# Lightning attention and a PReLU MLP on one core: converting transfers for q of chunk 1, and a new order of the whole list of calls

## The chip, the cores and the metric

The kernel runs on one core of one Trainium2 chip. The metric is device time in microseconds (us). Three runs of the kernel before took 202.56, 203.06 and 203.26 us, a median of 203.06.

The engines are named as in the profile: PE is TensorE (matrix products and transposes), with PEld for its weight loads; DVE is VectorE, ACT is ScalarE, POOL is GpSimd, and SP is the engine that only issues transfers here. PSUM is the memory that PE writes its products to; the other memory on the core is SBUF.

## What is computed

The reference has two parts. The first is linear attention with a decay for each head, in blocks of 64 positions, for 4 batches, 8 heads, 768 positions and a head dimension of 64. The result, x, has 3072 rows of 512, and goes through a two-layer MLP (512 to 2048 to 512) with a PReLU whose slope is given for each of the 2048 columns.

```python
for b in range(nb):                                   # blocks of 64 positions
    intra = einsum('bhic,bhjc->bhij', qb, kb) * Dmask[None]
    intra = einsum('bhij,bhjd->bhid', intra, vb)
    inter = einsum('bhid,bhde->bhie', qb * lam_pow[None], kv_state)
    out[:, :, sl] = intra + inter
    kb_dec = kb * rev_pow[None]
    kv_state = lam_block * kv_state + einsum('bhsd,bhse->bhde', kb_dec, vb)
...
h = x @ w_in
g = np.maximum(h, 0.0) + alpha * np.minimum(h, 0.0)
return (g @ w_out).astype(np.float32)
```

The inputs and the output are of 32-bit floats; the kernel multiplies in 16 bits.

## The kernel before, in words

**Tiles.** The rows are cut into six chunks, c = 0 to 5. A chunk holds 256 positions of two batches, 512 rows of x. Its attention is done in four units, one for each batch `bi` and half of the heads `hh`; so there are 24 units, and units 4c to 4c+3 make chunk c. Blocks are taken 128 positions at a time, two in a unit.

**A unit of attention** goes through these steps, each a small function:
- q, k and v are loaded. `load` (L89) brings q or k as 32-bit numbers into a raw tile, from the queue of SP or, with "G", of GpSimd; `cast` (L247 on ACT, L249 on DVE, L251 on GpSimd) makes 16 bits of it. `load_q16` (L279) and `load_v16` (L288) are converting transfers on GpSimd's queue, which read 32-bit numbers and write 16-bit ones, so that no cast is needed. `load_q16` puts a unit's q into its tile with the heads in another order.
- q and k are transposed. For units 0 to 8 PE does it (`turn`), into a bank of PSUM, and `turn_copy` copies the bank to `qkT` (L247 on ACT, L249 on DVE). Where q came by `load_q16`, `turn` does a unit's q with eight transposes of 64 columns (L334), else with four of 128 (L336). For units 9 to 23 a transfer on SP's queue transposes (`turned`).
- `key_decayed` multiplies k by its decay: one instruction on DVE or GpSimd (L308), or eight on ACT (L306), one for each head and parity. `decayed` (L361) does the same for q.
- `score_products` (L397, 16 small products) writes the scores into the one buffer `s` in PSUM; `masked` (L408, DVE) multiplies them by the mask of decays into `sm`, which frees `s`. `intra` (L422) multiplies them by v, `inter` (L381) multiplies q by the state, both into `acc`. `state_products` (L442), or `state_in` (L492 and L442) in a bank of its own, makes the next state's sum, and `first_state` (L469, ACT) or `states` (L477, DVE, two instructions for each block) adds it to the decayed state.
- `attended` copies `acc` to the tile xT (L247 on ACT, L249 on DVE), where the MLP reads it.

**The MLP.** `up(c, f)` (L518) multiplies w_in by a chunk's xT, for one of 16 groups f of 128 columns, into one of four banks of PSUM: four products of 512 columns, or of 256 where only one batch is ready (`up(0, 4, 0)`). `relu` (L531, ACT) makes relu(-h), and `prelu` or `prelu_half` (L546, DVE) adds it, times 1 - alpha, to h, which gives g in 16 bits. For chunk 0 `down` (L554) is the plain second product. For chunks 1 to 5 the second product is done in the manner of Strassen, in seven products instead of eight (`second`, L675, 256 columns each, tile names y and b), which need sums and differences of quarters of g (`g_sum`) and w_out (`w_sum`). For chunks 4 and 5 the up product is done the same way, as they are taken together (`first`, L800, tile names a, e and b), with sums of w_in (`in_sum`) and of the two chunks' xT (`x_sum`, i = 1 to 4, for each of two groups of rows). All these sums are one instruction each on L593 (a difference) or L596 (a sum), on DVE or, with "G", on GpSimd. `first(f, 5)` needs `x_sum(1, ...)`, which needs the first half of the heads only, unit 22 at the latest.

**The order.** All is called from one list, written out by hand from line 819 on: 1079 calls, each of which issues its instructions at once. Every engine runs its own instructions in the order of the list, and waits where data or a buffer isn't ready. `vector_turn(n)` marks the newest DVE instruction, and `gpsimd_waits(n)` makes the newest GpSimd instruction wait for that mark. `fill` (L133, 512 columns) and `tick` (L145, 128 columns) are products that nobody reads, ahead of the first transposes. The list ends with the second products of chunks 4 and 5.

```python
def turn(n, xs):                       # cut
    ...
        if x == 0 and "q16" in t:
            for l in range(2):
                nc.tensor.transpose(tp[ds(64 * l, 64), i, e, hp, :], t["q16"][:, 2 * hp + l, e], ident)
            continue
        nc.tensor.transpose(tp[:, i, e, hp, :], t["qk16"][:, x, e, ds(2 * hp, 2)]..., ident)
```

Of the kernel before, what the change touches and what calls it, by code (L numbers as in the profile page):

```python
# [11 lines left out]
def kernel(  # L12
# [489 lines left out]
    G = {}  # L502
# [316 lines left out]
    query_decay(3, 1)  # L819
    query_decay(2, 1)  # L820
    mask_logs(2)
    tick(6)
    load_q16(2)
    mask_logs(0)
    key_decay()
    state_decay()
    load(0, 0, "k", None)
    load(0, 1, "k", None)
    cast(0, "k16", "V")
    query_decay(0, 1)  # L830
    load_q16(0)
    load_q16(1)
    key_decayed(0, "V")
    mask_logs(1)
    key_decayed(1, "V")
    decay_mask(2)
    decay_mask(0)
    cast(1, "k16", "V")
    vector_turn(0)
    tick(56)  # L840
    load_q16(3)
    load_v16(1)
    decay_mask(1)
    mask_logs(3)
    query_decay(1, 1)
    turn(1, (1,))
    turn_copy(1, (1,), "V")
    decay_mask(3)
    query_decay(0, 0)
    load_alpha()  # L850
    load_v16(0)
    turn(1, (0,))
    turn_copy(1, (0,), "V")
    load_v16(2)
    turn(0, (1,))
    turn_copy(0, (1,), "V")
    turn(0, (0,))
    turn_copy(0, (0,), "A")
    load_v16(3)
    load_win(1)  # L860
    slopes_turn()
    slopes()
    load_win(0)
    decayed(1, "P")
    score_products(1)
    masked(1)
    fill(3)
    key_decayed(2)
    gpsimd_waits(0)
    cast(2, "k16", "A")  # L870
    turn(2, (0,))
    turn_copy(2, (0,), "V")
    state_in(1, 0)
    first_state(1)
    decayed(2)
    cast(3, "k16", "A")
    decayed(0)
    score_products(0)
    masked(0)
    turn(2, (1,))  # L880
    turn_copy(2, (1,), "A")
    key_decayed(3)
    inter(1)
    intra(1)
    attended(1, "A")
    load_win(3)
    turn(3, (0,))
    turn_copy(3, (0,), "A")
    state_in(0, 0)
    first_state(0)  # L890
    load(1, 0, "q", 0, "G")
    score_products(2)
    masked(2)
    turn(3, (1,))
    turn_copy(3, (1,), "A")
    state_in(2, 0)
    first_state(2)
    decayed(3)
    load(1, 0, "k", 0, "G")
    load(1, 0, "q", 1, "G")  # L900
    load_win(2)
    inter(0)
    intra(0)
    attended(0, "A")
    load_v16(4)
    load(1, 0, "k", 1, "G")
    state_in(1, 1)
    states(1, (1,))
    load_wout(0)
    score_products(3)  # L910
    masked(3)
    state_in(3, 0)
    first_state(3)
    inter(2)
    intra(2)
    attended(2, "A")
    load(1, 1, "q", 1, "G")
    state_in(2, 1)
    states(2, (1,))
    state_in(3, 1)  # L920
    states(3, (1,))
    state_in(0, 1)
    states(0, (1,))
    cast(4, "q16", "G")
    inter(3)
    intra(3)
    attended(3, "A")
    up(0, 4, 0)
    relu(0, 4, 0)
    up(0, 5)  # L930
    up(0, 3)
    up(0, 6)
    prelu_half(0, 4, 0)
    relu(0, 5)
    relu(0, 3)
    prelu(0, 5)
    up(0, 7)
    relu(0, 6)
    up(0, 13)
    prelu(0, 3)  # L940
    up(0, 15)
    relu(0, 7)
    prelu(0, 6)
    relu(0, 13)
    turn(4, (0,))
    relu(0, 15)
    prelu(0, 7)
    up(0, 14)
    load(1, 1, "k", 1, "G")
    prelu(0, 13)  # L950
    turn_copy(4, (0,), "A")
    up(0, 1)
    relu(0, 14)
    prelu(0, 15)
    cast(4, "k16", "G")
    turn(4, (1,))
    load_v16(5)
    load_wout(1)
    up(0, 0)
    prelu(0, 14)  # L960
    cast(5, "q16", "A")
    up(0, 4, 1)
    turn_copy(4, (1,), "A")
    relu(0, 1)
    relu(0, 4, 1)
    cast(5, "k16", "G")
    load(1, 1, "q", 0, "G")
    up(0, 9)
    key_decayed(4, "V")
    state_products(4, None, True)  # L970
    in_sum(1, 1, "G")
    score_products(4)
    load_wout(2)
    prelu(0, 1)
    prelu_half(0, 4, 1)
    relu(0, 0)
    relu(0, 9)
    turn(5, (0,))
    cast(7, "q16", "G")
    up(0, 12)  # L980
    relu(0, 12)
    first_state(4)
    load_wout(3)
    prelu(0, 0)
    w_sum(1, 1, "G")
    decayed(4)
    up(0, 2)
    turn_copy(5, (0,), "V")
    relu(0, 2)
    turn(5, (1,))  # L990
    prelu(0, 9)
    up(0, 11)
    relu(0, 11)
    prelu(0, 12)
    prelu(0, 2)
    key_decayed(5)
    turn_copy(5, (1,), "V")
    up(0, 8)
    gate(2, "out")
    prelu(0, 11)  # L1000
    load(1, 1, "k", 0)
    relu(0, 8)
    up(0, 10)
    prelu(0, 8)
    down(0, 2, 0)
    down(0, 0, 0)
    states(4, (1,))
    inter(4)
    masked(4)
    relu(0, 10)  # L1010
    down(0, 3, 0)
    intra(4)
    score_products(5)
    cast(6, "q16", "A")
    cast(7, "k16", "G")
    decayed(5)
    state_products(5)
    prelu(0, 10)
    w_sum(1, 3)
    in_sum(1, 2)  # L1020
    vector_turn(1)
    turn(7, (0,))
    load_v16(7)
    load_v16(6)
    first_state(5)
    down(0, 2, 1)
    in_sum(1, 3, "G")
    gpsimd_waits(1)
    turn_copy(7, (0,), "V")
    w_sum(2, 3, "G")  # L1030
    down(0, 3, 1)
    load_v16(8)
    states(5, (1,))
    attended(4, "A")
    decayed(7, "V")
    vector_turn(2)
    load(2, 0, "k", 0)
    turn(6, (0,))
    turn_copy(6, (0,), "V")
    w_sum(1, 0)  # L1040
    masked(5)
    down(0, 0, 1)
    w_sum(2, 1)
    turn(7, (1,))
    inter(5)
    w_sum(4, 1)
    key_decayed(7, "V")
    decayed(6, "V")
# [879 lines left out]
```

## Time and profile before

| | us |
|---|---|
| median of three runs | 203.06 (202.56 to 203.26) |
| the profiled execution, its own time | 203.85 |
| its span, first to last instruction | 202.1 |
| PE busy | 194.8, 96% of the span |
| DVE busy | 171.8, 85% |
| POOL busy | 142.1, 70% |
| ACT busy | 130.1, 64% |
| granted clock of TensorE, mean | 0.999 of full speed |

The busy times overlap, and PE's weight loads (130.0) run beside its products. In a row of a timeline stand the start in us from the span's start, the length, the engine, the line, the operation, the tiles written and read, their sizes and types, and the number of instructions joined in the row; a bracket tells how long the engine had stood idle just before, and which instruction the profile takes for the one that ended it. In a row of the waits stand the engine and line that waited, the engine and line waited for, the sum, the number of times and the longest. In the chain stand start, length and what ran. In a row of the groups by line stand, behind the bar, the busy time of the group and the mean length of one instruction in ns, and then the idle time before it with what ended most of it. In a row of the transfers stand their number, the size of each, and the median time from issue to landing.

### The profile page before, as it was taken

To read this page: it belongs to the slowest core of one execution; us is meant where nothing else is said; L and a number is where in the kernel's file an instruction comes from. 1 tells how busy PE (TensorE), PEld (TensorE's weight loads), DVE (VectorE), ACT (ScalarE), POOL (GpSimd) and SP (SyncE) were. 2 spreads that over 40 slices of the span, in tenths; PEclk is the share of its full clock that TensorE was granted. 3 is DMA by queue.
4 is the path that set the end of the run, shared out by engine and by line. 5 is a ranking of instruction groups with operands and counts; after the bars stand their busy time and mean duration, and the time that the engine had idled before them with its cause. 6 is when DMAs were issued, how large, how long until landed. Compare 5 with 4: busy or idle time off the path is not lost.

```text
span 202.1 us, 5896 instructions
## 1 busy us (share of the span) xinstructions
PE 194.8 (96%) x2367; PEld 130.0 (64%) x2367; DVE 171.8 (85%) x319; ACT 130.1 (64%) x279; POOL 142.1 (70%) x160
## 2 busy tenths in 40 slices
PE   7997999999999999999999999998999999999992
PEld 7965454556545688666556667655666656788891
DVE  6887789869989999899999998899989999895800
ACT  5585686336977799687768588364596986633022
POOL 8989959773889839999999989870476222656700
PEclk9999999999999999999999999999999999999999
DMA  5999999999989999999996935110040001113143
GB/s 156 199 198 230 239 260 234 200 278 235 235 127 248 228 199 238 164 280 142 262 207 161 185 26 136 67 63 0 2 156 3 0 2 54 55 34 122 55 143 117
DMA packets 60991, 30.01 MB, mean 149 GB/s; under 512 B 31700, under 2 KB 60004, under 8 KB 60964
## 3 DMA queue, kind: packets, MB, share of 16 engines
q1 hardware_dynamic: 41236, 19.87, 40.7%
q0 software_dynamic: 19568, 9.70, 36.1%
q8 instruction: 18, 0.29, 0.6%
q14 instruction: 9, 0.07, 0.1%
q10 hardware_dynamic: 160, 0.07, 0.1%
HBM read 27.27 MB, written 6.29 MB: 166 GB/s over the span
## 4 chain that ended last, share of the span: by engine, by line
PE 91%; DVE 4%; ACT 3%; issue 0%; ACTq 0%; DVEq 0%
PE h_ps L518 27%; PE y L675 16%; PE b L675 12%; PE o_ps L554 7%; PE b L800 5%; PE acc L422 4%; PE s L397 3%; PE a L800 3%; PE e L800 3%; PE unread L145 3%; PE acc L381 2%; PE tp L336 2%; PE acc L442 1%; DVE x L593 1%; ACT xT L247 1%; PE tp L334 1%
## 5 line engine op out<-in xcount | busy, mean ns | idle before, releaser
L518 PE MATMUL h_ps<-xT,w_in_sb 128*128 128x512 f16 (+1 forms) x264 | 59.5, 373 | 1.0 <-DVE g L546 1.0
L675 PEld LDWEIGHTS <-g 128*128 128x128 f16 x464 | 44.6, 98 | 10.5 <-DVE g L593 1.1
L546 DVE SCALAR_TENSOR_TENSOR g<-m,oma,h_ps 128x512 f16<-128x512 f32 (+1 forms) x66 | 46.1, 727 | 4.9 <-ACT m L531 3.5
L531 ACT ACTIVATE m<-h_ps 128x512 f32<-128x512 f32 (+1 forms) x66 | 37.4, 582 | 16.5 <-PE h_ps L518 15.6
L518 PEld LDWEIGHTS <-w_in_sb 128*128 128x128 f16 x264 | 24.5, 98 | 26.2 <-DVE g L546 1.3
L408 DVE TENSOR_TENSOR sm<-s,dmask 128x1024 f16<-128x1024 f32 x24 | 29.3, 1219 | 1.5 <-PE s L397 1.4
L675 PE MATMUL y<-w_out_sb,g 128*128 128x256 f16 x224 | 27.9, 273 | 0.6 <-DVE g L593 0.6
L593 POOL TENSOR_TENSOR g<-g 128x512 f16<-128x512 f16 x11 | 13.2, 1204 | 16.0 <-DVE s L596 15.9
L361 POOL TENSOR_TENSOR qdT<-qkT,qdecay 128x512 f16<-128x512 f16 (+1 forms) x20 | 20.8, 1043 | 3.2 <-DMA qkT<-qk 1.2
L675 PE MATMUL b<-t,g 128*128 128x256 f16 x160 | 19.8, 273 | 0.0
L288 POOL DMA_DIRECT2D v<-in_v_dram x24 | 18.6, 783 | 0.0
L247 ACT ACTIVATE xT<-acc 128x512 f16<-128x512 f32 x22 | 13.1, 595 | 8.2 <-PE acc L442 5.1
L593 POOL TENSOR_TENSOR g<-g,g 128x512 f16<-128x512 f16 x12 | 14.1, 1190 | 5.5 <-DVE g L593 3.3
L477 DVE SCALAR_TENSOR_TENSOR R<-R,rdecay,acc 128x128 f16<-128x128 f16 x54 | 15.6, 342 | 2.8 <-ACT xT L247 2.2
L596 POOL TENSOR_TENSOR s<-g,g 128x512 f16<-128x512 f16 x9 | 10.4, 1158 | 8.4 <-DVE g L546 8.4
L554 PE MATMUL o_ps<-w_out_sb,g 128*128 128x512 f16 x64 | 15.3, 380 | 0.0
L247 ACT ACTIVATE o_sb<-y 128x512 f32<-128x512 f32 (+2 forms) x12 | 6.2, 526 | 13.0 <-PE y L717 7.1
L308 POOL TENSOR_TENSOR kdec<-kraw,kdecay 128x512 f16<-128x512 f32 x13 | 13.6, 1054 | 0.8 <-DVE w_out_sb L593 0.8
L306 ACT ACTIVATE kdec<-kraw,kdecay 128x64 f16<-128x64 f32 x56 | 14.0, 344 | 0.0
L251 POOL CAST qk<-kraw 128x512 f16<-128x512 f32 x10 | 6.1, 608 | 5.9 <-DMA kraw<-in_k_dram 2.4
L422 PE MATMUL acc<-sm,v 64*64 64x128 f16 x384 | 9.9, 220 | 0.1
L397 PE MATMUL s<-qkT 64*64 64x128 f16 x384 | 9.9, 219 | 0.0
(133 smaller groups left out, 368.7 us busy)
## 6 DMA issues: line engine op xcount, KB each, us to landing
out_dram<-o_sb SPq DMA_DIRECT2D x23, 256.0 KB, 2.5
kraw<-in_k_dram SPq DMA_DIRECT2D x8, 512.0 KB, 5.8
v<-in_v_dram POOLq DMA_DIRECT2D x24, 128.0 KB, 5.2
qraw<-in_q_dram SPq DMA_DIRECT2D x5, 512.0 KB, 6.5
w_in_sb<-in_moe_w_in_dram POOLq DMA_DIRECT2D x4, 512.0 KB, 7.5
w_out_sb<-in_moe_w_out_dram POOLq DMA_DIRECT2D x4, 512.0 KB, 9.4
qraw<-in_q_dram SPq DMA_DIRECT2D x6, 256.0 KB, 5.5
kraw<-in_k_dram SPq DMA_DIRECT2D x5, 256.0 KB, 4.5
```

The costliest lines, as they stand in the source:

```text
L247: nc.scalar.activation(out, in_, AF.Copy)
L288: nc.gpsimd.dma_start(out=v16.rearrange("p h e d -> p h (e d)"), in_=v[2 * (c % 2) + bi, ds(4 * hh, 4), ds((c // 2) * W, W), :].rearrange( ...
L361: engine(eng).tensor_tensor(out=qdT[:, :, :, p], in0=(t["qps"] if eng == "P" else t["qkT"][:, 0])[:, :, :, p], in1=qdecay[:, hh, :, :, p], ...
L408: nc.vector.tensor_tensor(out=t["sm"].rearrange("p a h x j -> p (a h) x j"), in0=t["s"].rearrange("p a h x j -> p (a h) x j"), in1=mask_of ...
L422: nc.tensor.matmul(ot[a][ds(hl * 64, 64), hp, :], lhsT=t["v16"][p, 2 * hp + hl, e, :], rhs=t["sm"][p, hl, hp, 1 - e, :], start=(2 * pb + a ...
L518: nc.tensor.matmul(h[:, 0:n] if bi is None else h[:, 0:n].rearrange("p (e j) -> p e j", e=2), lhsT=w_in_sb[:, gi, ts(f, 128)], rhs=x.rearr ...
L531: nc.scalar.activation(m[:, 0:n], HP[c, f, bi][:, 0:n], AF.Relu, scale=-1.0)
L546: engine(eng).scalar_tensor_tensor(out=g, in0=m, scalar=oma[:, f : f + 1], in1=h, op0=ALU.mult, op1=ALU.add)
L554: nc.tensor.matmul(O[c, t], lhsT=g_of(c, f)[:, t // 2, t % 2, :], rhs=w_out_sb[:, f, :], start=(f == 0), stop=(f == NF - 1),)
L593: engine(eng).tensor_tensor(out=out, in0=a, in1=b, op=ALU.subtract)
L675: nc.tensor.matmul(Y[c, k][:, ds(b * HALF, HALF)], lhsT=left(c, i, f, b), rhs=right(i, f), start=(f == 0 and b == 0 and i in (1, 5)), stop ...
L800: nc.tensor.matmul(t, lhsT=w, rhs=x, start=(g == 0 and i in (1, 5)), stop=(g == 1), skip_group_check=True)
```

## The change

Only the list is changed; every function is the same. It has 1078 calls for 1079.

First, q of chunk 1 (units 4 to 7). Before it came by four plain loads on GpSimd's queue and four casts, two on GpSimd and two on ACT; now by four converting transfers. `turn` then takes its other branch for these units, eight transposes of 64 columns for four of 128, 16 more on PE in all.

```diff
-    load(1, 0, "q", 0, "G")
-    load(1, 0, "q", 1, "G")
-    load(1, 1, "q", 1, "G")
-    load(1, 1, "q", 0, "G")
-    cast(4, "q16", "G")
-    cast(5, "q16", "A")
-    cast(7, "q16", "G")
-    cast(6, "q16", "A")
+    load_q16(4)
+    load_q16(7)
+    load_q16(5)
+    load_q16(6)
...
-    key_decayed(2)
-    gpsimd_waits(0)
-    cast(2, "k16", "A")
+    key_decayed(3, "V")
+    vector_turn(0)
```

Second, the order is new nearly everywhere from the first call to the second products of the last chunk, whose tail is the same on each engine. With it some work goes to other engines. On ACT `key_decayed` is done for 11 units, before for 7. On DVE the differences of L593 go from 54 to 48 and the sums of L596 from 37 to 34, on GpSimd both together from 55 to 64. DVE does five copies of `attended` and four casts, before two and three. There are 25 calls of `gpsimd_waits`, before 22, and 18 of `vector_turn`, as before.

The first place that the prediction speaks of is DVE at the first four units. L249 copies transposes (`qkT`) or makes xT (CAST), L361 is `decayed`, L408 `masked`, L308 `key_decayed`, L477 `states`, and L237 makes 1 - alpha. Before:

```order
L195 SCALAR_TENSOR_TENSOR dmask<-rel_f,loglam,drop 128x192 x2
L249 COPY qkT<-tp 128x512 x3
L237 TENSOR_SCALAR oma<-at_ps 128x16
L361 TENSOR_TENSOR qdT<-tp,qdecay 128x4x64
L408 TENSOR_TENSOR sm<-s,dmask 128x1024
L249 COPY qkT<-tp 128x512
L408 TENSOR_TENSOR sm<-s,dmask 128x1024 x2
L477 SCALAR_TENSOR_TENSOR R_1_2_101<-R_1_1_100,rdecay,kv 128x128 x2
L408 TENSOR_TENSOR sm<-s,dmask 128x1024
```

After, at the same place:

```order
L249 COPY qkT<-tp 128x512
L308 TENSOR_TENSOR kdec<-kraw,kdecay 128x512
L249 COPY qkT<-tp 128x512
L361 TENSOR_TENSOR qdT<-tp,qdecay 128x4x64
L249 COPY qkT<-tp 128x512
L408 TENSOR_TENSOR sm<-s,dmask 128x1024
L249 COPY qkT<-tp 128x512
L408 TENSOR_TENSOR sm<-s,dmask 128x1024
L249 CAST xT<-acc 128x2x4x64
L408 TENSOR_TENSOR sm<-s,dmask 128x1024
L237 TENSOR_SCALAR oma<-at_ps 128x16
L477 SCALAR_TENSOR_TENSOR R_0_2_104<-R_0_1_103,rdecay,kv 128x128 x2
```

The fourth masking is the next row in the list after. A `key_decayed` now stands between the first two copies, a copy to xT between the second and the third masking, and the slopes and a pair of states ahead of the fourth.

The second place is DVE at the last masking, of unit 23, where attention ends and the up products of chunks 4 and 5 begin. Here `g0` to `g3` are a chunk's g, `s1` to `s4` sums of w_in (or of g, for s1 on L596), and `x1`, `x2`, `x4` the sums of xT. Before:

```order
L408 TENSOR_TENSOR sm_3017<-s_2955,dmask_175 128x1024
L546 SCALAR_TENSOR_TENSOR g3_2629<-m_3020,oma_182,h_ps_3010 128x512
L593 TENSOR_TENSOR g2_2242<-g2_2242,g0_2079 128x2x256
L593 TENSOR_TENSOR x1_3071<-xT_2808,xT_2438 128x512
L593 TENSOR_TENSOR x2_3076<-xT_2808,x1_3071 128x512
L593 TENSOR_TENSOR x4_3078<-xT_2438,x2_3076 128x512
L593 TENSOR_TENSOR g3_1978<-g3_1978,g1_2035 128x2x256
L593 TENSOR_TENSOR g0_2386<-g0_2386 128x2x256
L593 TENSOR_TENSOR x2_3076<-xT_2808,x1_3071 128x512
L593 TENSOR_TENSOR g3_1978<-g3_1978,g1_2035 128x2x256
```

After:

```order
L408 TENSOR_TENSOR sm_3062<-s_3000,dmask_175 128x1024
L593 TENSOR_TENSOR s4_3064<-w_in_sb_121,s2_2030 128x512
L593 TENSOR_TENSOR x1_3066<-xT_2896,xT_2442 128x512
L593 TENSOR_TENSOR s4_3064<-w_in_sb_121,s2_2030 128x512
L596 TENSOR_TENSOR s1_1652<-g0_2489,g2_2464 128x512
L593 TENSOR_TENSOR x1_3066<-xT_2896,xT_2442 128x512
L593 TENSOR_TENSOR s4_3064<-w_in_sb_121,s2_2030 128x512
L546 SCALAR_TENSOR_TENSOR g3_2662<-m_3116,oma_182,h_ps_3068 128x512
L546 SCALAR_TENSOR_TENSOR g1_2722<-m_3079,oma_182,h_ps_3048 128x512
L593 TENSOR_TENSOR x2_3134<-xT_2896,x1_3066 128x512
```

Both halves of x1 are made on DVE now (before, one of them on GpSimd), ahead of two PReLUs and of x2; the sums of g for the second product of chunk 2 no longer stand among them. On PE, between the last `intra` and the first `first(1, 1)`, stand `second(2, 4, 1)` and `second(2, 3, 0)` now, before `second(2, 4, 1)` alone.

More of the change, by code (lines that the diff above doesn't have):

```diff
@@ L995 @@
[L995 to L1011, printed above, removed]
+    up(0, 8)
+    turn(7, (0,))
+    load_v16(6)
+    turn_copy(7, (0,), "V")
+    turn(6, (0,))
+    relu(0, 11)
     intra(4)
     score_products(5)
-    cast(6, "q16", "A")
-    cast(7, "k16", "G")
@@ L1158 @@
+    cast(11, "q16", "A")
     load_v16(12)
[L1159 to L1182 removed]
+    load(3, 1, "q", 0)
+    relu(1, 13)
@@ L1342 @@
+    up(2, 12)
+    up(2, 1)
+    states(13, (0, 1))
+    cast(18, "q16", "A")
+    second(1, 4, 0)
+    masked(13)
+    relu(2, 12)
+    relu(2, 1)
+    load_v16(19)
+    inter(13)
+    key_decayed(16, "A")
+    intra(13)
+    prelu(2, 12)
+    prelu(2, 1)
+    decayed(14)
+    load(4, 0, "q", 0)
+    state_products(14)
     score_products(14)
+    up(2, 13)
+    second(1, 4, 1)
+    masked(14)
     prelu(2, 2)
-    intra(13)
-    state_products(14)
-    relu(2, 12)
+    attended(13, "A")
+    states(14, (0, 1))
```

1656 lines of the change are left out of this document (826 added, 830 removed).

## The prediction

> **What bounds the kernel now.** I read the page's totals first, then the span in windows, then the list of waits with TensorE as the one that waits, then the chain that ended last and the timeline at the two places where TensorE waits. First the page.
>
> ```profile
> span 202.1 us, 5896 instructions
> PE 194.8 (96%) x2367; PEld 130.0 (64%) x2367; DVE 171.8 (85%) x319; ACT 130.1 (64%) x279; POOL 142.1 (70%) x160
> PE 91%; DVE 4%; ACT 3%; issue 0%; ACTq 0%; DVEq 0%
> ```
>
> TensorE (PE) is busy for 194.8 of 202.1 us and carries 91% of the chain. So a new order can win only from the 7.3 us in which PE stands, and it loses whatever matmuls it adds. The windows say where those 7.3 us lie (behind the length come the busy times of PE, of its weight loads, and of DVE, ScalarE and GpSimd).
>
> ```profile
> 0.00:5.00 5.00, 3.88 (x34) 3.59 (x35) 3.44 (x15) 2.83 (x8) 4.16 (x14) 1.00 0.55 154
> 15.00:20.00 5.00, 3.83 (x121) 2.70 (x112) 4.01 (x11) 2.71 (x6) 4.98 (x8) 1.00 1.23 223
> 110.00:120.00 10.00, 10.00 (x145) 6.91 (x143) 9.99 (x20) 7.02 (x14) 9.01 (x10) 1.00 0.71 107
> 130.00:140.00 10.00, 9.09 (x75) 5.51 (x74) 9.21 (x18) 4.85 (x10) 5.23 (x5) 1.00 0.16 54
> 196.00:202.10 6.10, 2.13 (x24) 1.79 (x21) 0.00 (x0) 1.36 (x3) 0.00 (x0) 0.96 0.34 114
> ```
>
> 1.12 us at the start, 1.17 in 15 to 20, 0.91 in 130 to 140 and 3.97 behind the last product make 7.17 of the 7.3. The start and the end belong to set-up and to the last store; the order of the first two microseconds and of the tail stays the same on each engine, so I leave both at zero. What a new list can touch is the 1.17 and the 0.91, and VectorE (DVE), which is 9.99 busy of 10 in 110 to 120 without PE yet losing anything there. The list of waits names what PE waited for in the later one; the row of the earlier one (19.37) is shown in part 2.
>
> ```profile
> PE y L675 <- DVE g L593: 0.6, 1, 0.6
> PE e L800 <- DVE x L593: 0.3, 1, 0.3
> ```
>
> **Part 1, eight short transposes for four long ones.** Units 4 to 7 are concerned; the chain has one group of each form side by side.
>
> ```profile
> 8.66 0.22 PE tp L336 x4
> 8.88 0.34 PE tp L334 x8
> 9.22 0.33 PE tp L336 x4
> ```
>
> Four of 128 columns take 0.22, eight of 64 take 0.34, so a unit costs 0.12 more, and four units 4 x 0.12 = +0.48. They stand between up-products, where PE is the bound, so nothing hides them. The other group of four took 0.33; by that one the term would be 4 x 0.01 = +0.04. I take 0.48, since 0.22 is a group that follows others without a break, and keep both ends. The four casts that go (two on GpSimd, two on ScalarE) were on engines with 30% and 36% free: nothing.
>
> **Part 2, the first units.** The list of the first four units is new. Before, it ran like this on DVE and PE.
>
> ```profile
> 6.66 0.68 DVE L308 TENSOR_TENSOR kdec<-kraw,kdecay 128x512 f16<-128x512 f32 x1
> 8.92 1.10 DVE L249 COPY qkT<-tp 128x512 f16<-128x512 f16 x3 [0.59 <-PE tp L336]
> 10.54 1.22 DVE L408 TENSOR_TENSOR sm<-s,dmask 128x1024 f16<-128x1024 f32 x1
> 12.28 1.23 DVE L408 TENSOR_TENSOR sm<-s,dmask 128x1024 f16<-128x1024 f32 x1 [0.19 <-PE s L397]
> 14.02 1.23 DVE L408 TENSOR_TENSOR sm<-s,dmask 128x1024 f16<-128x1024 f32 x1 [0.52 <-PE s L397]
> 15.46 0.61 DVE L477 SCALAR_TENSOR_TENSOR R<-R,rdecay,kv 128x128 f16<-128x128 f16 x2 [0.21 <-PE kv L442]
> 15.98 1.22 DVE L408 TENSOR_TENSOR sm<-s,dmask 128x1024 f16<-128x1024 f32 x1
> 18.82 0.48 DVE L546 SCALAR_TENSOR_TENSOR g<-m,oma,h_ps 128x256 f16<-128x256 f32 x1
> 3.28 5.37 PE unread L145 x62
> 10.41 0.75 PE unread L133 x3
> 17.48 0.38 PE acc L422 x16
> 17.88 0.60 ACT xT L247
> 19.37 1.90 PE L518 MATMUL h_ps<-xT,w_in_sb 128*128 128x512 f16 x8 [1.01 <-DVE g L546]
> ```
>
> Follow the four maskings (L408), which carry the chain there.
> - Ahead of the first transposes stand 56 small fillers and the three large ones, for 62: three large take 0.75, six small 6 x 5.37/62 = 0.52, so the first copy begins at 8.92 + 0.23 = 9.15.
> - Between the two copies of unit 1 now stands a key_decayed of unit 3, 0.68 with the next instruction 0.6 behind it. So the second copy begins at 9.15 + 0.35 + 0.6 = 10.1 (0.35 is a third of the 1.10), scores follow at 10.45 and last some 0.4. The first masking starts at about 11.15, for 10.54: +0.6.
> - The second masking waits for scores in the one buffer that the first empties; the distance of 1.74 stays: 12.9, for 12.28, +0.6.
> - Ahead of the third scores PE now has intra of unit 1, a state product and the transposes of unit 3; PE reaches them at about 14.3, not 13.6: 14.7 to 15.0, for 14.02.
> - Ahead of the fourth stand the slopes and one pair of states (0.61): 16.8 to 17.6, for 15.98, +0.8 to +1.6.
>
> Behind the fourth masking come intra (0.38), the copy to xT (0.60) and then up(0,5), the first product that needs all four units. In the trace xT ends at 17.88 + 0.60 = 18.48; up(0,5) began at 19.37, after a wait of 1.01. Moving 18.48 by 0.8 to 1.6 gives 19.3 to 20.1. So the wait that is there hides nearly the whole delay: -0.1 to +0.7, and I take the middle, +0.3. If that cover is none (the wait moves along), it is a rival below. GpSimd's loads are moved too. Of the four of w_in three are issued earlier than before, and the last, w_in(2), behind seven other issues of 0.77 each, at about 20.5 by the trace's GpSimd rows.
>
> ```profile
> w_in_sb<-in_moe_w_in_dram POOLq DMA_DIRECT2D x4, 512.0 KB, 7.5
> 16.69 0.77 POOL L89 DMA_DIRECT2D kraw<-in_k_dram x1
> ```
>
> It lands near 28.0. Its first reader, up(0,9), comes behind eleven up-products of four times 0.216 (0.86 each), so at 19.7 + 9.5 = 29.2 at the earliest: nothing, with 1.2 us of cover; if that were gone PE would stand for what is missing.
>
> **Part 3, the change from attention to the last two chunks.** Here PE lost time in two steps.
>
> ```profile
> 134.15 1.37 DVE L593 TENSOR_TENSOR x<-xT 128x512 f16<-128x512 f16 x1
> 136.90 0.42 DVE L593 TENSOR_TENSOR x<-xT,x 128x512 f16<-128x512 f16 x1
> 134.89 0.38 PE L800 MATMUL e<-x,s 128*128 128x512 f16 x1
> 135.57 0.81 PE L800 MATMUL e<-x,s 128*128 128x512 f16 x3 [0.30 <-DVE x L593]
> 136.22 0.88 PE L675 MATMUL y<-w_out_sb,g 128*128 128x256 f16 x6
> 137.71 0.39 PE L675 MATMUL y<-w_out_sb,g 128*128 128x256 f16 x2 [0.61 <-DVE g L593]
> 133.90 1.33 POOL L593 TENSOR_TENSOR s<-w_in_sb,s 128x512 f16<-128x512 f16 x1
> 31.82 2.59 PE h_ps L518 x12
> ```
>
> A product of 512 columns takes 2.59/12 = 0.216, so the second e could start at 135.11, and started at 135.57: 0.46 lost. Six of 256 columns, at half of that each, take 6 x 0.108 = 0.65, so the next y could start at 136.87, and started at 137.71: 0.84 lost. Together 1.3. After the change the sums x(1), which need only units already copied, stand on DVE directly behind the last masking and behind at most two other sums (0.42 each) apiece; the sums of g for second(2,4) are done on GpSimd and DVE ahead of them; and between the last intra and the first e PE has two groups of second products (8 x 0.108 = 0.86 each) and two of first products (4 x 0.216 each). From the end of the last masking DVE needs about 5 x 0.34 = 1.7 us for both x(1), while PE has 0.38 + 1.73 + 1.73 = 3.8 us of work. The next sum, x(2), follows two PReLUs (0.66 each) by DVE at about 3.7, with PE, which does four more e first, at 4.7. No wait is left: -1.3. Bounds: 0 (the wait moves to a later sum) to -1.3.
>
> **Part 4, who does what.** GpSimd takes over 9 sums of two inputs, ScalarE four key_decayed of eight scalings, DVE one copy of a cast and three of xT.
>
> ```profile
> L593 POOL TENSOR_TENSOR g<-g,g 128x512 f16<-128x512 f16 x12 | 14.1, 1190 | 5.5 <-DVE g L593 3.3 <-DVE g L546 1.3 <-PE y L675 0.9
> L306 ACT ACTIVATE kdec<-kraw,kdecay 128x64 f16<-128x64 f32 x56 | 14.0, 344 | 0.0
> L593 DVE TENSOR_TENSOR t<-w_out_sb,t 128x512 f16<-128x512 f16 x6 | 3.1, 514 | 0.0
> ```
>
> GpSimd gains 9 x 1.19 = 10.7 and loses four casts and three key_decayed; ScalarE gains 32 x 0.344 = 11 of its 72 free us; DVE loses 9 x 0.42 = 3.8 (a sum alone) and gains some 3 x 0.60 + 0.42 = 2.2 (the copies at ScalarE's 0.60). Neither GpSimd nor ScalarE limits a stretch of the trace (9.01 of 10 is GpSimd's share in 110 to 120), so I cost this at nothing, between -0.4 and +1.9. The lower end: where DVE is a little late, eight products of 512 columns take 1.83 instead of 8 x 0.216 = 1.73, and four such places would make 0.4.
>
> ```profile
> 117.31 1.83 PE h_ps L518 x8
> ```
>
> The upper end is two collisions as in 134.15: the sum took 1.37 beside GpSimd's 1.33 and 0.42 alone, 0.95 more. The three waits of GpSimd that are added (25 for 22) hold its queue behind a DVE instruction; behind them stand GpSimd's sums and loads. GpSimd stands idle for 60 us of the span, so such a wait costs only where a sum is needed within about a microsecond.
>
> [...]
>
> **Sum.** +0.48 + 0.3 - 1.3 + 0 = -0.5. The profiled execution took 203.85 for a span of 202.1; its 1.75 us around the span stay. That run lies 0.8 above the median of 203.06. I move the median by the same amount: 203.06 - 0.5 = 202.5. About 0.3%, 0.6 us, is what a measurement of this kernel can tell from no change.
>
> **Rivals.**
> - A, faster still. Part 2 at its lower end (-0.1) and part 4 at -0.4 give 0.48 - 0.1 - 1.3 - 0.4 = -1.3, so 201.7. For it: DVE, 9.99 of 10 busy, gets work taken off. Against it: PE lost little in that window.
> - B, the gain of part 3 is half lost. The y behind x(1) now waits for another sum, one that GpSimd makes in 1.19 and DVE would in 0.42, 0.77 later: 203.06 - 0.5 + 0.6 = 203.2, no change that can be told. For it: one of the two waits was for a sum of g, and sums of g move to GpSimd. Against it: GpSimd was only 5.23 busy of 10 there.
> - C, slower: up(0,5) does wait for the first PReLU, as the row of 19.37 says, and not for xT alone. Then nothing is hidden. In the new list that PReLU stands on DVE behind three pairs of states which follow the fourth masking. With that masking at 17.6, intra ends near 19.1, xT near 19.75, the first relu near 20.4, PReLU at 20.95, and up(0,5) starts at about 21.0: +1.6. The sum becomes 1.6 + 0.48 - 1.3 = +0.8, so 203.9. It decides from a fourth masking at about 17.2 on. Against it: in the program that product waits for xT and states, and shares no tile with the PReLU.
> - D, slower by the collisions of part 4: two where PE waits for DVE, 2 x 0.95 = +1.9, -0.5 + 1.9 = +1.4, so 204.4. One of them would already undo the gain.
>
> The order shows that the edit itself does what it says: on PE 16 more transposes, on GpSimd four converting loads of q. I keep no rival for that.
>
> **How the numbers follow.** The likeliest case, 202.5, has a chance of 0.34 and a range of its own from 202.0 to 202.9; the bound of 0.3% (202.45) cuts it in half. A has 0.24, B 0.16, C 0.14, D 0.12. Faster: 0.17 + 0.24 = 0.41, same: 0.17 + 0.16 = 0.33, slower: 0.14 + 0.12 = 0.26. The range goes from 201.3 (A with the transposes at +0.04) to 204.1 (C with part 2 a little later); D and what lies under A stay out, some 0.17.
>
> **What would show it.** In the profile after: the first four L408 of DVE at about 11.2, 12.9, 14.8 and 17.2, and up(0,5) (the first h_ps of 512 columns on PE) at 19.7; a start at 21 with a PReLU ending just ahead of it would be C. Groups of eight L334 in units 4 to 7, 0.34 each. No wait of e or y for DVE at the first L800 products; a wait there for POOL would be B. DVE sums over a microsecond beside PE idle times would be D. I am wrong altogether if PE idles by over half a microsecond anywhere between 25 and 130 us, where it had no wait before.

## The result, and the profile after

The median went from 202.99 us (202.56 to 204.05) to 205.67 us (203.01 to 207.94), 18 runs each. The ratio is 1.0061, with a 95% interval of 1.0032 to 1.0090, slower by more than a measurement can miss, with eight runs of the new kernel left out that lie over 1.5% above its fastest; the medians here are of all runs, since those eight are slow through the kernel itself. In 11 of its 18 runs the mean granted clock is below 0.994, in the kernel before in 6 of the 114 runs beside the experiments (the profiled execution, with 3.4 us at half clock, has 0.992). The other 7 runs took 203.01 to 203.37 (four) and 204.56 to 204.80 (three).

The page of the profiled execution (206.11 us, clock 0.992), of which I show the totals:

```profile
span 204.3 us, 5963 instructions
PE 196.0 (96%) x2383; PEld 130.8 (64%) x2383; DVE 169.8 (83%) x312; ACT 135.2 (66%) x307; POOL 147.7 (72%) x163
```

The work moved as counted: DVE 2.0 less, ACT 5.1 and POOL 5.6 more. The timeline of DVE at the first four units, after:

```profile
9.11 0.43 DVE L249 COPY qkT<-tp 128x512 f16<-128x512 f16 x1 [1.64 <-PE tp L336]
...
11.05 1.21 DVE L408 TENSOR_TENSOR sm<-s,dmask 128x1024 f16<-128x1024 f32 x1
12.85 1.23 DVE L408 TENSOR_TENSOR sm<-s,dmask 128x1024 f16<-128x1024 f32 x1 [0.26 <-PE s L397]
14.79 1.22 DVE L408 TENSOR_TENSOR sm<-s,dmask 128x1024 f16<-128x1024 f32 x1
16.93 1.21 DVE L408 TENSOR_TENSOR sm<-s,dmask 128x1024 f16<-128x1024 f32 x1
18.06 1.62 DVE L477 SCALAR_TENSOR_TENSOR R<-R,rdecay,kv 128x128 f16<-128x128 f16 x6
21.50 0.48 DVE L546 SCALAR_TENSOR_TENSOR g<-m,oma,h_ps 128x256 f16<-128x256 f32 x1 [1.81 <-ACT m L531]
```

The four maskings stand where the prediction put them (11.15, 12.9, 14.7 to 15.0, 16.8 to 17.6). The last copy to xT ends at 19.26, just ahead of the forecast (19.3 to 20.1). What PE does then was not forecast. PE's timeline at the first up-products, and ACT's last copy to xT:

```profile
18.55 0.50 PE L518 MATMUL h_ps<-xT,w_in_sb 128*128 128x256 f16 x3
20.68 7.44 PE L518 MATMUL h_ps<-xT,w_in_sb 128*128 128x256 f16 x29 [1.63 <-issue]
18.66 0.60 ACT L247 ACTIVATE xT<-acc 128x512 f16<-128x512 f32 x1 [0.55 <-PE acc L422]
```

PE stops for 1.63 us in the middle of `up(0, 4, 0)`, behind its third product, at a place where no data can be missing: all four products read weights of one load and the xT of units 0 and 1, which three of them have used. xT is done at 19.26, PE goes on at 20.68. The releaser is "issue", none that the profile shows, and the first PReLU comes later, at 21.50. Then the windows of 1 us (the third column from the end is the granted clock):

```profile
20.00:21.00 1.00, 0.32 (x2) 0.25 (x2) 0.00 (x0) 0.00 (x0) 0.99 (x2) 0.72 1.55 253
21.00:22.00 1.00, 1.00 (x4) 0.29 (x2) 0.48 (x1) 0.38 (x1) 0.69 (x1) 0.50 1.40 250
23.00:24.00 1.00, 1.00 (x4) 0.39 (x3) 0.58 (x1) 0.68 (x2) 1.00 (x3) 0.57 1.43 297
24.00:25.00 1.00, 1.00 (x7) 0.47 (x5) 0.22 (x2) 0.60 (x1) 0.98 (x2) 1.00 1.41 206
```

From about 20.44 to 23.85 the clock is at half: 3.4 us, in which PE does 1.7 us of work. So 1.3 us of later start and 1.7 us of half clock cost 3.0, where the two profiled executions differ by 2.3 (206.11 for 203.85). From PE's restart to the end before took 202.1 - 19.37 = 182.7, after 204.3 - 20.68 - 1.7 = 181.9: the rest is about 0.8 better. That is the 0.48 - 1.3 that was forecast against this execution of before, but partly by luck, since a new wait of 0.49 (at 128.87, below) is in it too. The waits of part 3 are gone; PE's timeline at the first products of chunks 4 and 5 has none:

```profile
137.67 1.04 PE L675 MATMUL y<-w_out_sb,g 128*128 128x256 f16 x8
138.55 1.03 PE L800 MATMUL a<-xT,w_in_sb 128*128 128x512 f16 x4
139.41 0.59 PE L800 MATMUL e<-x,s 128*128 128x512 f16 x2
```

**What the stop is.** The page, of before as of after, has a queue for instructions, with its transfers, their MB and their share:

```profile
q8 instruction: 18, 0.29, 0.6%
```

That is 16 KB each (16384 bytes in the trace's list of packets). In that list one of them begins at 17.10 in before and at 18.47 in after, and takes 0.96 us. In both, PE's records (products, weight loads and a few others, counted in order) stop behind number 705 and go on 1.31 and 1.25 us after that transfer ends. So my theory 1: PE runs out of instructions, which come in blocks, and in after the block comes later. That a block is 256 is an estimate of mine from the trace of before: its 2367 products and 2367 weight loads, over 18 transfers, make 263 to each, and 256 would make 18.5 blocks; the block that ends with 705 then begins behind 449. Theory 2, the rival: PE waits there for data.

### The profile page after: what moved, and what is told of

It is laid out like the page before. It is cut to its first block, busy times and chain, and to the rows that moved or that the text cites. A ratio compares the mean times of both kernels' runs of the same rounds, so it can differ in the third digit from the quotient of the medians.

```text
span 204.3 us, 5963 instructions
## 1 busy us (share of the span) xinstructions
PE 196.0 (96%) x2383; PEld 130.8 (64%) x2383; DVE 169.8 (83%) x312; ACT 135.2 (66%) x307; POOL 147.7 (72%) x163
## 4 chain that ended last, share of the span: by engine, by line
PE 91%; DVE 4%; ACT 2%; issue 1%; ACTq 0%
PE h_ps L518 28%; PE y L675 16%; PE b L675 12%; PE o_ps L554 7%; PE b L800 5%; PE acc L422 4%; PE e L800 3%; PE a L800 3%; PE s L397 3%; PE unread L145 2%; PE acc L381 2%; DVE sm L408 2%; PE acc L442 1%; PE tp L336 1%; PE tp L334 1%
## 5 line engine op out<-in xcount | busy, mean ns | idle before, releaser
L518 PE MATMUL h_ps<-xT,w_in_sb 128*128 128x512 f16 (+1 forms) x264 | 62.0, 380 | 1.6 <-issue 1.6
L675 PEld LDWEIGHTS <-g 128*128 128x128 f16 x464 | 45.0, 98 | 10.0 <-DVE g L546 0.2
L408 DVE TENSOR_TENSOR sm<-s,dmask 128x1024 f16<-128x1024 f32 x24 | 29.2, 1217 | 4.4 <-PE s L397 4.4
L361 POOL TENSOR_TENSOR qdT<-qkT,qdecay 128x512 f16<-128x512 f16 (+1 forms) x21 | 22.0, 1052 | 3.8 <-DVE qkT L249 1.4
L306 ACT ACTIVATE kdec<-kraw,kdecay 128x64 f16<-128x64 f32 x88 | 22.1, 336 | 0.3 <-DMA kraw<-in_k_dram 0.3
L675 PE MATMUL b<-t,g 128*128 128x256 f16 x160 | 20.3, 273 | 0.0
L593 POOL TENSOR_TENSOR g<-g,g 128x512 f16<-128x512 f16 x12 | 14.1, 1188 | 5.2 <-PE y L675 4.2
L596 POOL TENSOR_TENSOR s<-g,g 128x512 f16<-128x512 f16 x10 | 11.5, 1155 | 8.0 <-DVE g L546 8.0
L247 ACT ACTIVATE xT<-acc 128x512 f16<-128x512 f32 x19 | 11.3, 596 | 7.7 <-PE acc L442 4.3
L477 DVE SCALAR_TENSOR_TENSOR R<-R,rdecay,acc 128x128 f16<-128x128 f16 x54 | 15.5, 339 | 0.5 <-ACT xT L247 0.4
L554 PE MATMUL o_ps<-w_out_sb,g 128*128 128x512 f16 x64 | 14.7, 379 | 0.0
L593 POOL TENSOR_TENSOR g<-g 128x512 f16<-128x512 f16 x9 | 10.3, 1155 | 2.6 <-DVE s L596 2.6
L308 POOL TENSOR_TENSOR kdec<-kraw,kdecay 128x512 f16<-128x512 f32 x10 | 10.7, 1066 | 1.8 <-DVE t L593 1.4
L554 PEld LDWEIGHTS <-g 128*128 128x128 f16 x64 | 6.0, 98 | 6.4
```

What stands on the lines that cost most here:

```text
L306: nc.scalar.activation(kdec[:, e, h], kr[:, e, h], AF.Copy, scale=kdecay[:, x, e : e + 1])
L361: engine(eng).tensor_tensor(out=qdT[:, :, :, p], in0=(t["qps"] if eng == "P" else t["qkT"][:, 0])[:, :, :, p], in1=qdecay[:, hh, :, :, p], ...
L408: nc.vector.tensor_tensor(out=t["sm"].rearrange("p a h x j -> p (a h) x j"), in0=t["s"].rearrange("p a h x j -> p (a h) x j"), in1=mask_of ...
L518: nc.tensor.matmul(h[:, 0:n] if bi is None else h[:, 0:n].rearrange("p (e j) -> p e j", e=2), lhsT=w_in_sb[:, gi, ts(f, 128)], rhs=x.rearr ...
L554: nc.tensor.matmul(O[c, t], lhsT=g_of(c, f)[:, t // 2, t % 2, :], rhs=w_out_sb[:, f, :], start=(f == 0), stop=(f == NF - 1),)
L593: engine(eng).tensor_tensor(out=out, in0=a, in1=b, op=ALU.subtract)
```

## The experiments

All were timed against the kernel before on the same chip; "distance" is from PE's instruction 449 to the start of that transfer. Low clock means a run below 0.994.

| kernel | 449 | transfer | stop behind 705 ends at (wait shown) | low clock | median |
|---|---|---|---|---|---|
| before | 14.35 | 17.10 | 19.37 (1.01) | 6 of 114 | 203.0 |
| after | 14.68 | 18.47 | 20.68 (1.63) | 11 of 18 | 205.67 |
| after, load_win(3) behind decayed(2) | 14.64 | 17.00 | 19.24 (0.23) | 1 of 12 | 203.29 |
| before, load_win(3) early | 14.20 | 17.90 | 20.12 (1.90) | 5 of 12 | 204.86 |
| after, loads of chunk 1 later | 14.37 | 18.26 | 20.66 (1.92) | 4 of 6 | 206.38 |
| before, load_win(3) later | 14.46 | 17.07 | 19.29 (0.81) | 1 of 12 | 202.98 |
| after, load_win(3) behind decayed(3) | 13.94 | 17.08 | 19.36 (1.04) | 1 of 12 | 204.16 |
| before, load_win(0) later | 14.22 | 15.33 | no stop | 1 of 12 | 204.43 |
| after, load_win(0) later | 13.71 | 15.79 | 18.27 (0.19) | 1 of 12 | 205.24 |

**Fewer PE instructions ahead.** In after, and in the same way in before:

```diff
-    tick(56)
+    tick(8)
...
-    fill(3)
+    fill(22)
```

> The kernel after, but 48 of the 56 small fillers are replaced by 19 large ones of the same length together (48 x 0.087 = 4.2 us, 19 x 0.217 = 4.1 us). PE so has 58 instructions fewer ahead of the attention (each filler is a weight load and a product), and nothing else changes. Theory 1, PE's instructions arrive too late: in both traces PE stops behind its instruction 705, in before until 1.31 us after the end of a 16 KB transfer of the instruction queue (17.10 + 0.96), in after until 1.25 us after it (18.47 + 0.96), and the stop of 1.63 us in after is what lets the clock fall to half for 3.4 us. With 58 instructions fewer ahead, instruction 705 is the 29th product behind that place, about 6 us of up-products later, so the transfer has landed by then. Expected: no stop of over 0.4 us between 18 and 22 us, granted clock 1.00 in every run, median 201.9 to 202.7. Theory 2, PE waits there for data (a PReLU, a state, a weight load): the stop of 1.0 to 1.6 us stays at the same product, some runs have a clock of 0.99, median 204 to 206.

> The kernel before with the same exchange of 48 small fillers for 19 large ones. Theory 1 (instructions too late): the stop of 1.01 us ahead of the first up-product of 512 columns, at 18.36 to 19.37, goes, and that product starts when xT is ready, near 18.5; median 202.99 less 0.9, so 202.1. Theory 2 (data): the stop stays and the time is that of before, 203.0.

Medians 203.79 (203.22 to 206.18; low clock in 3 of 12, where the expectation had none) and 203.12 (202.68 to 203.63). PE's timelines, first of after with large fillers, then of before with them, and last of before itself:

```profile
19.57 0.42 PE L422 MATMUL acc<-sm,v 64*64 64x128 f16 x16
19.92 4.28 PE L518 MATMUL h_ps<-xT,w_in_sb 128*128 128x256 f16 x23
```

```profile
16.30 0.22 PE L442 MATMUL kv<-v,kdec 64*64 64x64 f16 x2 [0.62 <-issue]
18.80 5.58 PE L518 MATMUL h_ps<-xT,w_in_sb 128*128 128x256 f16 x27
```

```profile
17.76 0.61 PE L518 MATMUL h_ps<-xT,w_in_sb 128*128 128x256 f16 x4
```

The stop at the up-products is gone from both, though PE's data are the same. This alone leaves theory 2 a way out, since PE comes to these products 1.4 and 1.0 us later than in after and before (19.92 for 18.55, 18.80 for 17.76), and data that land meanwhile would no longer stop it. But in before a stop of 0.62 us now stands at a place that had none, behind instruction 449, 256 ahead of 705, which has moved into the small products of attention and whose block arrived at 14.89, 1.4 us ahead of PE's restart. The stop follows the number of the instruction, not the data: theory 2 falls. The time did not fall: the 22 large fillers of after took 5.78 us, 0.26 each for the 0.217 of the expectation, and the trace doesn't show why; so everything started later (the first masking of after at 12.03, not 11.05; in before, whose 19 took 4.26, the first scores at 10.36, not 9.99). The stop was moved, not removed.

**What lowers the clock.** After with large fillers, with `attended(3, "A")` called four times:

> The kernel after with the large fillers, and the copy of unit 3 to xT made four times on ScalarE instead of once (the same values again), 0.5 us each: PE then has to wait for data ahead of the first up-product of 512 columns, about 1.5 us longer. This asks what lets the clock fall. Theory 1a, any idle time of PE of this length does: PE stands for about 1.7 us near 19, and in a third or more of the runs the granted clock is 0.98 to 0.993; these take 205 to 207, the others 203.5 to 204.2. Theory 1b, only the stop for instructions does, or another cause in those runs: the clock stays 1.00 in all runs, median the large fillers' own plus 1.5.

PE's timeline:

```profile
22.57 1.67 PE L518 MATMUL h_ps<-xT,w_in_sb 128*128 128x512 f16 x7 [1.61 <-ACT xT L247]
```

The same idle time, but for data: low clock in 3 of 6 runs (0.973 to 0.992, 206.96 to 208.45); the others 205.44 to 205.88. So a wait for data goes with the low clock too, as 1a says; but the same kernel without that wait had it in 3 of 12 runs, and six runs can't tell the one share from the other, so 1a is not shown. In the trace of after the granted clock fell to 0.50 at 20.44 and stayed there for 3.4 us; ahead of that PE had been idle for 0.34 us, up to 17.88, and for 1.4 from 19.05 on. The length of the stop alone doesn't decide it: the profiled executions of this kernel (1.61) and of before with `load_win(3)` early (1.90) kept the full clock (mean 1.00 in both). What decides which run is hit, no run shows.

**Part 1 alone**, in before:

```diff
-    load(1, 0, "q", 0, "G")
+    load_q16(4)
...
-    cast(4, "q16", "G")
```

> The kernel before with part 1 of the change alone: q of units 4 to 7 by converting transfers at the places of the plain loads, without the four casts. The prediction's term: eight short transposes take 0.12 us more than four long ones in each unit, +0.48, so 203.5, and the groups of L334 in the trace of units 4 to 7 last 0.34 each. Its lower bound: +0.04. Rival: the converting transfers change when the instruction transfer near 17.1 us starts; then the start of the first up-product of 512 columns moves by as much as that transfer, up to 1.4 us.

Median 203.52, ratio 1.0028 (1.0001 to 1.0056). From its timeline of PE, against before:

```profile
29.61 0.41 PE L334 MATMUL tp<-ident,qk 128*64 128x128 f16 x8
29.96 1.90 PE L518 MATMUL h_ps<-xT,w_in_sb 128*128 128x512 f16 x8
```

A group of eight takes 29.96 - 29.61 = 0.35 and in before a group of four 0.23: 0.12 a unit, as forecast, and +0.5 in the time. The transfer of instructions started at 17.06, not moved: the converting loads are not what holds it up.

**What holds the instructions up.** GpSimd's issues of the first three loads of w_in, in before and then in after; the third of them is `load_win(3)`:

```profile
8.74 1.54 POOL L98 DMA_DIRECT2D w_in_sb<-in_moe_w_in_dram  x2
14.49 0.79 POOL L98 DMA_DIRECT2D w_in_sb<-in_moe_w_in_dram  x1
```

```profile
8.73 0.81 POOL L98 DMA_DIRECT2D w_in_sb<-in_moe_w_in_dram  x1
10.75 1.49 POOL L98 DMA_DIRECT2D w_in_sb<-in_moe_w_in_dram  x2
```

Two kernels move that load, each to about where the other list has it, and a third moves other loads:

```diff
     load_win(0)
...
-    load_win(3)
     key_decayed(2)
     decayed(0)
...
     decayed(2)
+    load_win(3)
```

in after; in before the other way round,

```diff
     load_win(0)
+    load_win(3)
...
     attended(1, "A")
-    load_win(3)
```

and in after the five loads of chunk 1:

```diff
-    load(1, 0, "k", 0, "G")
...
-    load_q16(4)
...
-    load(1, 0, "k", 1, "G")
...
+    up(0, 6)
+    load(1, 0, "k", 0, "G")
+    load_q16(4)
+    load(1, 0, "k", 1, "G")
     load_q16(7)
     load_q16(5)
-    up(0, 6)
```

> The kernel after, with one load of w_in, load_win(3), moved on GpSimd's queue from ahead of key_decayed(2) to behind decayed(2), which is about where it stands in the kernel before. In the traces the 16 KB transfer that brings the instructions behind number 705 starts 2.75 us after PE has begun instruction 449 in before (14.35 to 17.10), and 3.79 us after it in after (14.68 to 18.47). Theory 1c, that transfer waits behind the loads of weights that are under way, of which after issues one more by then: the distance falls to about 2.8 us, the stop behind instruction 705 from 1.63 to under 1.0 us, the clock is below 0.994 in fewer than 1 run of 4 (11 of 18 in after), median 203.2 to 203.7. Theory 1d, the distance comes from other traffic (the loads of chunk 1) or from chance: distance 3.3 to 4, clock below 0.994 in about half of the runs, median 204.5 to 206.

> The kernel before, with load_win(3) issued directly behind load_win(0), about 4 us earlier and where after has it. Theory 1c (the instruction transfer waits behind loads of weights): it starts about 3.8 us behind instruction 449, not 2.75; PE's stop behind 705 grows from 1.0 to about 2.0 us; the clock is below 0.994 in a third or more of the runs, and the median is 204 to 206. Theory 1d: distance 2.5 to 3, stop of 1.0, clock 1.00 in nearly all runs, median 203.0.

> The kernel after, with the five loads of q and k of chunk 1 that GpSimd issues from 15.7 us on moved behind the call of up(0, 6). Theory 1d (these loads hold the instruction transfer up): distance from instruction 449 to the transfer under 3 us, stop under 1.0 us, clock below 0.994 in fewer than 1 run of 4, median 203.2 to 203.7, unless their later landing costs units 4 to 7 a wait. Theory 1c (the loads of weights, issued from 8.7 to 12.2 us, hold it up): distance still 3.3 to 4, clock low in about half of the runs, median 204.5 to 206.

PE's timelines of the first two, in this order:

```profile
18.51 0.50 PE L518 MATMUL h_ps<-xT,w_in_sb 128*128 128x256 f16 x3
19.24 5.02 PE L518 MATMUL h_ps<-xT,w_in_sb 128*128 128x256 f16 x25 [0.23 <-issue]
```

```profile
17.61 0.61 PE L518 MATMUL h_ps<-xT,w_in_sb 128*128 128x256 f16 x4
20.12 4.06 PE L518 MATMUL h_ps<-xT,w_in_sb 128*128 128x512 f16 x18 [1.90 <-DVE g L546]
```

One load of weights, issued 2.9 us later in after and 4.3 us earlier in before, carries the loss from the one list to the other: after falls to 203.29 (ratio 1.0012, 0.9985 to 1.0039), before rises to 204.86 (1.0080, 1.0052 to 1.0108). The low clock goes with it: 1 run of 12 for 11 of 18, and 5 of 12 for 6 of 114. The loads of chunk 1 have no such part: with these issued later the transfer still started at 18.26, and the median was 206.38. That is 1c. Note the bracket in the last row: it names the PReLU as releaser as in before, in a kernel where a 16 KB transfer moved PE's start.

**Later still.** `load_win(3)` behind `decayed(3)`, in both lists (in before together with the first load of q of chunk 1):

> The kernel before, with load_win(3) and the first load of q of chunk 1 moved behind decayed(3) on GpSimd's queue, some 1.5 us later. If the transfer of instructions waits behind loads of weights, the distance from instruction 449 to its start (2.75 in before, 3.70 with load_win(3) early) falls to 1.5 to 2.3 us, PE's stop behind 705 from 1.0 to 0.2 to 0.6 us, and the median to 202.2 to 202.6. If only loads issued before 14 us count, the distance stays at 2.7 and the median at 203.0.

> The kernel after, with load_win(3) behind decayed(3), one more step later than behind decayed(2). Distance from instruction 449 to the transfer 1.5 to 2.3 us (2.36 there, 3.79 in after), no stop beyond 0.3 us behind 705, clock 1.00 in nearly all runs, median 202.9 to 203.3, that is the time of before: the gains and losses of the rest of the new list cancel.

Medians 202.98 (ratio 1.0007, 0.9979 to 1.0035) and 204.16 (1.0029, 1.0005 to 1.0054). The transfer stayed at 17.07 and 17.08: the second outcome of the first expectation, and the other one missed. In the packet lists the loads of w_in run one behind the other, the first two until about 17.0, and the instructions come right then. So the second, `load_win(0)`, is moved as well, here in before; in after it goes behind `decayed(2)`, and `load_win(3)` behind `decayed(3)` as above:

```diff
-    load_win(0)
...
     key_decayed(3)
+    load_win(0)
...
-    load_win(3)
...
-    load(1, 0, "q", 0, "G")
...
     decayed(3)
+    load_win(3)
+    load(1, 0, "q", 0, "G")
```

> The kernel before, with load_win(0) moved from about 9.5 to about 14.4 us on GpSimd's queue, behind key_decayed(3), and load_win(3) and the first load of q of chunk 1 behind decayed(3). In all traces so far the first two loads of w_in are carried one behind the other until 17.0 to 17.15 us, and the instruction transfer starts at 17.0 at the earliest. If it waits for loads that were issued before PE began instruction 449 (14.3 us), only one is left: the transfer starts at 14.5 to 15.5, PE doesn't stop behind 705, the first up-product of 512 columns starts when xT is ready, near 18.5, and the median is 202.2. If something else holds it until 17.0, or the load of w_in that is now later keeps up(0, 3) waiting, the stop stays at 1.0 or moves, and the median is 203.0 or more.

> The kernel after, with load_win(0) behind decayed(2) and load_win(3) behind decayed(3). If the stop is all that is wrong with the new list: the instruction transfer starts by 15.5, no stop behind 705, up(0, 5) waits for xT until 19.3 only, clock 1.00 in nearly all runs, and the median is 202.9 to 203.2, since the stop was 0.2 us already in the run with load_win(3) behind decayed(2) (203.1). If the rest of the list is the better one, as forecast, it comes out below 202.6.

The transfer started at 15.33 and 15.79, and there is no stop, or 0.19. But PE's timeline of before with it:

```profile
17.64 1.47 PE L518 MATMUL h_ps<-xT,w_in_sb 128*128 128x256 f16 x8
19.96 2.76 PE L518 MATMUL h_ps<-xT,w_in_sb 128*128 128x512 f16 x12 [0.85 <-DMA w_in_sb<-in_moe_w_in_dram]
23.82 1.90 PE L518 MATMUL h_ps<-xT,w_in_sb 128*128 128x512 f16 x8 [1.10 <-DMA w_in_sb<-in_moe_w_in_dram]
```

Now the weights are late: 0.85 + 1.10 us, medians 204.43 and 205.24. The cause of the stop is settled, the remedy isn't this one: in these orders either PE's instructions or its weights come late.

**The early sums**, part 3 alone, in before, and with `load_win(3)` or `load_win(0)` later. Each call is taken from its later place, where `x_sum(1, 0)` was on GpSimd:

```diff
     masked(23)
+    x_sum(1, 0)
+    x_sum(1, 1)
+    g_sum(2, 4, 0, 1)
+    g_sum(2, 4, 1, 0)
+    g_sum(2, 4, 1, 1)
...
-    x_sum(1, 0, "G")
...
```

> The kernel before with part 3 of the change alone: both sums x(1) on VectorE directly behind the last masking, and the three sums of g for the second product of chunk 2 behind them, ahead of x(2) and x(4). The prediction's term: PE's waits for e and y there go, -1.3, so 201.7. Rival: the trace that the term was taken from was of an execution above the median (203.85 for 203.0), in which one sum took 1.37 us beside GpSimd; two other traces with this part of the list unchanged lose only 0.5 there, so -0.5, 202.5, or less if the sums moved up delay the PReLUs behind them.

> The two moves together: load_win(3) later, and the sums x(1) and of g directly behind the last masking. The gains should add, if they are what the traces say: the fast half of the runs of the early sums (202.2 to 202.65) less what the shorter stop gives, 0.4 to 0.8: the lowest runs near 201.6, the median 201.8 to 202.6, clock 1.00 in all or nearly all runs. If the early sums bring a loss of another kind in half of the runs, the times fall into two groups about 1.2 us apart.

> The same moves of loads with the early sums of x(1) and g. If both gains are there they add: lowest runs near 201.4, median 201.4 to 201.8, clock 1.00 in nearly all runs. If the stop stays: 202.4, as with the early sums and load_win(3) later alone.

Medians 203.03 (ratio 0.9995, 0.9966 to 1.0024), 202.42 (0.9968, 0.9939 to 0.9997) and 204.58 (1.0071, 1.0037 to 1.0106). The first fell into two groups, six runs of 202.20 to 202.65 and six of 203.42 to 204.65; the second had 10 of 12 runs in the lower group, 202.26 to 202.71, though its stop stayed as it was (19.28). The lower group is 0.5 below that of before (202.7 to 203.3). The middle one is the only version here that beats both kernels, by a little; whether the upper group really appears less often in it (2 of 12 for 6 of 12), twelve runs each don't tell.

Why 0.5 and not 1.3? DVE's timelines of before with large fillers (203.01) and of before with `load_win(3)` later (204.02), the same part of the list in both:

```profile
134.35 0.41 DVE L593 TENSOR_TENSOR x<-xT 128x512 f16<-128x512 f16 x1
```

```profile
134.40 1.37 DVE L593 TENSOR_TENSOR x<-xT 128x512 f16<-128x512 f16 x1
```

and of PE in them:

```profile
134.94 1.03 PE L800 MATMUL e<-x,s 128*128 128x512 f16 x4
136.96 0.39 PE L675 MATMUL y<-w_out_sb,g 128*128 128x256 f16 x2 [0.34 <-DVE g L593]
```

```profile
135.83 0.81 PE L800 MATMUL e<-x,s 128*128 128x512 f16 x3 [0.24 <-DVE x L593]
137.97 0.39 PE L675 MATMUL y<-w_out_sb,g 128*128 128x256 f16 x2 [0.62 <-DVE g L593]
```

One sum takes 0.41 in the one execution and 1.37 in the other, and with it PE loses 0.5 or 1.3 here. Of the six profiled kernels with this part of the list as in before, four have 0.41. The execution that the prediction was read from (203.85) was of the second kind; by its time the median of before is of the first.

## Why the prediction was wrong

It said 202.5, and the step that failed is in part 2: "GpSimd's loads are moved too", costed at "nothing, with 1.2 us of cover". I asked of the moved loads only when they land themselves. Nor are three of the four loads of w_in issued earlier, as the prediction has it, but one: they start at 8.73, 10.75, 11.48 and 21.30, before at 8.74, 9.47, 14.49 and 18.21. That one, the third, pushed back a transfer that I didn't count, that of PE's own instructions (18.47 for 17.10; 0.33 of this is PE's coming to instruction 449 later). Moving this one load back gives 203.29, moving it the other way in before gives 204.86. Behind it stands the misread wait: the 1.01 us at 19.37 was taken as slack that would hide a later xT, so the working had -0.1 to +0.7, taken as +0.3. It wasn't slack for data but a stop for instructions, and its end moved with their transfer: +1.3, and then the half clock, 1.7, which the prediction didn't have at all. With the load moved back the wait does hide the delay: 0.23 of it is left, and PE goes on at 19.24.

Point by point:
- **Part 1**, +0.48: right, +0.5 by itself.
- **Part 2**, the four maskings and xT: right to some 0.2 us (xT 19.26, forecast 19.3 to 20.1). The start of `up(0, 5)`: wrong, by the above. A stop there with no data behind it was not among the rivals. Rival C had the place, the sign and, by luck, nearly the price (21.0; PE went on at 20.68), but not the cause: the PReLU came at 21.50, after PE had gone on.
- **Part 3**, -1.3: the waits are gone as worked out; the size was that of one execution, whose time the prediction itself put 0.8 above the median. In the median of before the waits there are worth 0.5.
- **Part 4**, 0 between -0.4 and +1.9: inside the bounds, but not by the collisions that the upper one was made from. The new list has a wait of its own. PE's timeline of after, then GpSimd's:

```profile
127.36 1.03 PE L518 MATMUL h_ps<-xT,w_in_sb 128*128 128x512 f16 x4
128.87 0.38 PE L381 MATMUL acc<-qdT,R 128*128 128x128 f16 x4 [0.49 <-DVE g L546]
```

```profile
122.75 2.25 POOL L593 TENSOR_TENSOR s<-s,w_in_sb 128x512 f16<-128x512 f16 x2
125.44 2.27 POOL L593 TENSOR_TENSOR g<-g,g 128x512 f16<-128x512 f16 x2 [0.43 <-DVE g L593]
127.66 1.16 POOL L361 TENSOR_TENSOR qdT<-qkT,qdecay 128x512 f16<-128x512 f16 x1
```

`inter` (L381) reads qdT, which GpSimd makes behind four sums and ends at 128.82; the bracket names another instruction again. In after with `load_win(3)` behind `decayed(3)` (204.19) the same wait is 1.42, and the profile names the right one:

```profile
126.94 0.38 PE L381 MATMUL acc<-qdT,R 128*128 128x128 f16 x4 [1.42 <-POOL qdT L361]
```

So the gain of part 3 (0.5) is given back here (0.4 to 1.4), part 1 costs 0.5, and what is left without the stop is 203.29 for 202.99: no change that can be told. That the two groups of after's runs at full clock (203.0 to 203.4 and 204.6 to 204.8) differ by this wait, 0.4 or 1.4, is argued from the sizes alone: the one profiled execution of after itself is of neither. It fits that after with `load_win(3)` behind `decayed(2)`, profiled at 203.11 with nearly the same restart (19.24 for 19.36), has 0.43 there.

The range (201.3 to 204.1) missed the median since no case had the clock in it. The sign that the prediction named for being "wrong altogether", over half a microsecond of idle PE between 25 and 130 us, was just missed in this execution (0.49, at 128.87).

## What to carry to other kernels

A wait whose named releaser makes no sense in the program (an instruction that shares no tile with it, or "issue") need not be slack (here the 1.01 us at 19.37 was none): look at what else arrives then, the instruction queue among it, before using it as cover. A load moved earlier is not free because it lands early enough (here moving one such load back took 205.67 to 203.29); ask which other transfer then stands behind it. And where two executions of one kernel differ by as much as the gain one hopes for, a term read from a single profile has to be set against the median, by a second trace.

## What the hardware showed that was not expected

- PE's instructions come in transfers of 16 KB, 18 in the trace of before, and PE stood behind numbers 449 and 705, 256 apart. Where instructions are small PE outran the transfers here: in the kernels of the table, instructions 449 to 705 took 3.7 to 4.1 us, mostly in attention, against 0.96 to 1.37 us for the transfer, 1.25 to 1.47 us from its end to PE's next instruction where PE stopped, and 1.1 to 3.9 us from instruction 449 to its start. In before, from 105 us on, the same distance for the later blocks is 0.55 us or less (0.30 at 108.98, 0.55 at 133.43), with fewer loads under way: the DMA share was 0.90 in 105 to 110 and 0.71 or less behind it, for 1.23 in 15 to 20.
- In the kernels of the table the transfer started at 17.0 to 17.1 where the issue of two loads of w_in had begun by 10.8 us, at 17.9 to 18.5 where that of three had by 11.5, at 15.3 and 15.8 where that of one had. It didn't wait for the third one's end (20.7), and in after with large fillers, with three begun by 12.5, it started only 2.65 us behind instruction 449; so how the transfers share is not settled.
- Where PE stood for instructions for 1.6 to 1.9 us, 20 of 36 runs had the low clock (11 of 18, 5 of 12, 4 of 6); with the 1.0 us of before 6 of 114 had. In the trace of after the half clock lasted 3.4 us (mean of the span 0.992), in that of after with the loads of chunk 1 later 6.8 (0.980).
